# Who makes the low parts of the expert weights: GpSimd or VectorE

## The chip, the core and the metric

The kernel runs on one core of a Trainium2 chip. The core has TensorE (PE: matrix products, with PEld for loading the stationary operand), VectorE (DVE), ScalarE (ACT), GpSimd (POOL) and SyncE (SP), which work from queues of their own and wait for each other by semaphores. Each queue is taken strictly in order. The metric is the device time of one execution in microseconds; lower is better.

## The reference: what is computed

The program is a windowed attention over 8 batches (8 heads, 512 local and 32 global positions, head size 64), and behind it a layer of 8 experts. The attention's output is the matrix x of 4608 rows of 512. The routing is a capacity-limited one: all 4608 x 8 logits are taken from the largest down, and a token goes to the first expert that still has room (576 rows each).

```
logits = x @ w_gate
order = np.argsort(-logits.flatten())
for idx in order:
    tok, e = (int(idx) // E, int(idx) % E)
    if assigned[tok] >= 0 or counts[e] >= cap:
        continue
    assigned[tok] = e
    counts[e] += 1
...
for e in range(E):
    mask = assigned == e
    h = np.maximum(x[mask] @ w1[e], 0.0)
    out[mask] = h @ w2[e]
```

With w1[e] of 512 x 1024 and w2[e] of 1024 x 512, each expert costs two matrix products over 576 rows.

## The kernel before, in words

**Attention** comes first (about 235 us of the span), then the routing of the first expert alone, and then eight **phases**, one for each expert in the order in which experts fill up. `ffn(ph)` writes one phase. It has three stretches on TensorE:

- **H** (L851): 16 groups of 12 products, `hh = relu(w1 x)`, over 544 of the 576 rows and the rest in a small piece; 192 matmuls of 128x272. Each group is turned by ACT into `hh` (L853) and then by DVE into its low part `hl` (L405, out `hl`), and the PSUM buffer `H` (three of them) comes free when DVE is done.
- **P** (L869): 16 small matmuls for the last 32 rows.
- **Y** (L879): 4 tiles of 24 products against w2, 96 matmuls of 128x512, with two small ones (L885) behind the first tile. ACT takes each tile out (L824) and GpSimd scatters it to DRAM (L731).

**Split numbers.** To keep accuracy with the reduced-precision matmul type, each factor is used as a high and a low part, and a product is three matmuls (high x high, low x high, high x low). ACT makes the high part of a weight piece of 128x512 (`w1h`, `w2h`, L701, a copy to the reduced type), and another engine makes the low part `raw - high` (`w1l`, `w2l`, L702). Each expert has 8 pieces of w1 and 8 of w2. Before the change GpSimd makes the low parts, all but four pieces of the first expert, which DVE makes ahead of the phases.

**Weights and rows** arrive by indirect DMAs issued from GpSimd's queue: two of 1 MB for w1 (into `w1r`), two of 1 MB for w2 (into `w2r`), and five for the expert's rows of x (`xg`), which PE transposes (`trans_x`, L724), ACT copies (`xh`) and DVE splits (`xl`).

**Routing** of the next expert runs beside the phase. It is a chain that goes back and forth between PE and DVE. A search of 8 rounds finds the value at which an expert is full. A round is: 17 small matmuls and one more (`R`, L468) that count with the operand `r_G`; `r_ce` on DVE; two matmuls; the scan `r_pm` on DVE; and then the next `r_G`, a 128x544 operation on DVE. Behind the search come the expert's number (`widx`, which allows its weights to be fetched), the counts (`r_cs`, a matmul pair, `r_pos`), a compaction (`r_rhs`, `r_ohl`, 34 matmuls, `r_w`, one matmul) and the list of rows (`idx`, which allows `xg` to be fetched). The next search follows at once.

**What sets the order.** The program is written out ahead of time by a small planner in `experts`. `step(ns)` advances a clock `V.now` after every matmul; `Queue` (L383 to L406) adds an estimated cost for each DVE operation to `V.busy`; `routing` yields the value of `V.now` from which its next piece may be written; `todo` holds the other jobs with a time and a condition. In each `step` the first job that is due and whose condition holds is written, and then the routing goes on if its time has come. `calm` (L747) is the condition under which a low part may be written, and `pool_op` keeps the estimate for GpSimd's queue. So the places of matmuls, DVE operations and DMA issues in their queues come from these estimates, and the chip follows the queues.

Of the kernel before, what the change touches and what calls it, by code (L numbers as in the profile page):

```python
# [371 lines left out]
AHEAD = 200  # L372
# [10 lines left out]
class Queue:  # L383
# [12 lines left out]
    def __getattr__(s, name):  # L396
        op = getattr(s.eng, name)

        def issue(*args, **kw):
            aps = [x for x in list(args) + list(kw.values()) if hasattr(x, "dtype") and hasattr(x, "shape")]  # L400
            n = max(int(np.prod(x.shape[1:])) for x in aps)
            fast = name in ("tensor_scalar", "tensor_copy") or name == "tensor_tensor" and all(
                mybir.dt.size(x.dtype) == 2 for x in aps)
            s.busy = max(s.busy, s.now) + 130 + n * (0.55 if fast else 1.05)
            return op(*args, **kw)  # L405
        return issue  # L406

# [257 lines left out]
def experts(ctx, tc, A, xd, ident, rt, out):  # L665
    nc = tc.nc
# [33 lines left out]
    def split(hi, lo, raw, eng):  # L700
        nc.scalar.activation(hi, raw, AF.Copy)  # L701
        eng.tensor_tensor(lo, raw, hi, op=ALU.subtract)  # L702

    def split_w1(raws, j, eng):
        q = slice(512 * (j % 2), 512 * (j % 2) + 512)
        split(w1h[j // 2][:, q], w1l[j // 2][:, q], raws[j // 4][:, (j // 2) % 2, q], eng)

    def split_w2(j, eng):
        split(w2h[j], w2l[j], w2r[j // 4][:, j % 4], eng)
# [24 lines left out]
    V = rt.V  # L734
    V.now = V.busy = 0.0
    pool, dma, need = [0.0], [0.0], [0.0]
    fill, todo, raw1 = [], [], {}
    done, cur, mid, wrote = [False], [0], [-1], [0.0]

    def pool_op(ns, nbytes=0):  # L740
        pool[0] = max(pool[0], V.now) + ns
        if nbytes:
            dma[0] = max(dma[0], pool[0] + 1800) + nbytes / 360.0
            return dma[0] + 300
        return pool[0]

    def calm():  # L747
        return pool[0] < V.now + AHEAD

    def chain():  # L750
        for ph in range(1, E):
# [37 lines left out]
            bubble()  # L789

    def low1(p, j):
        split_w1(raw1[p], j, nc.gpsimd)
        pool_op(1225)

    def low2(j):
        split_w2(j, nc.gpsimd)
        pool_op(1225)

    def get_w1(p, half):
        raw1[p] = load_w1(p)  # L800
        r = [pool_op(1040, 1 << 20) for _ in range(2)]
        for i in range(4):
            at(f"a{p}", r[i // 2], lambda j=2 * i: low1(p, j), lambda: (half or mid[0] == p - 1) and calm())
        for i in range(4):
            at(f"b{p}", r[i // 2], lambda j=2 * i + 1: low1(p, j), lambda: mid[0] == p - 1 and calm())
# [7 lines left out]
    def get_w2(p):  # L813
        load_w2(p)
        r = [pool_op(1040, 1 << 20) for _ in range(2)]
        for j in range(8):
            at(f"w{p}", r[j // 4], lambda j=j: low2(j), lambda: cur[0] == p and calm())
# [93 lines left out]
    for j in range(4):  # L911
        at("b0", 0, lambda j=j: low1(0, 2 * j + 1), calm)
    for j in range(8):
        at("w0", 0, lambda j=j: low2(j), calm)
# [80 lines left out]
```

## Time and profile before

| | us |
|---|---|
| median of three timed runs | 792.48 (790.07 to 793.71) |
| the profiled execution, its own time | 788.45 |
| span of that execution | 786.7 |
| TensorE busy, by the page | 715.7 (91%) |
| VectorE busy | 487.2 (62%) |
| ScalarE busy | 312.9 (40%) |
| GpSimd busy | 319.6 (41%) |
| mean granted TensorE clock | 0.947 |

Times in the profile are counted from the start of the span. The first product of the first expert's H is at 276.7 us and the last product of the last expert's Y at 774.3. A "phase" below is the time from one expert's first H product to the next one's.

### The profile page before, as it was taken

Reading aid. Unit: us, or ns where it says so; the run is one execution under the profiler, and the core shown is the slowest. Engines: PE = TensorE matmul, PEld = TensorE weight load, DVE = VectorE, ACT = ScalarE, POOL = GpSimd, SP = SyncE. Lnnn points to the kernel's source line nnn. Section 1 sums busy time; section 2 is a strip of 40 time slices with the busy share of each in tenths; the row PEclk is TensorE's granted clock in tenths of the full one; section 3 lists DMA queues with packets and bytes.
Section 4 is the critical chain, followed back from the end, with each engine's and each line's share of the span. In section 5 each row is a group of like instructions: output and inputs, shape, how many; then the busy total and the mean of one; then the engine's idle time right before and its main releaser. Section 6 shows DMA issues by size and latency. Waiting matters only on the chain.

```text
span 786.7 us, 21184 instructions
## 1 busy us (share of the span) xinstructions
PE 715.7 (91%) x8636; PEld 579.5 (74%) x8636; DVE 487.2 (62%) x1705; ACT 312.9 (40%) x849; POOL 319.6 (41%) x314
## 2 busy tenths in 40 slices
PE   7999999999983499979997997999799999999993
PEld 6777777777751488769777876977777887988973
DVE  5887886778777887787758657666774731130210
ACT  4657675665640242342422423332331423443410
POOL 5221111111000471782746645553644655574510
PEclk9999999999995589998998999899999989999998
DMA  9999789878420520602332323132142313341000
GB/s 350 409 353 339 295 298 321 299 276 310 162 70 1 164 108 30 256 31 83 126 108 105 125 102 134 43 136 85 68 127 82 121 49 137 129 137 72 28 26 31
DMA packets 32417, 120.51 MB, mean 153 GB/s; under 512 B 6720, under 2 KB 6976, under 8 KB 24128
## 3 DMA queue, kind: packets, MB, share of 16 engines
q1 hardware_dynamic: 22080, 67.78, 23.2%
q0 software_dynamic: 10240, 51.39, 18.7%
q8 instruction: 68, 1.11, 0.6%
q14 instruction: 29, 0.24, 0.1%
HBM read 101.32 MB, written 17.83 MB: 151 GB/s over the span
## 4 chain that ended last, share of the span: by engine, by line
PE 79%; DVE 14%; issue 2%; DMA 2%; ACT 1%; POOL 0%; POOLq 0%; SPq 0%; ACTq 0%; DVEq 0%
PE Y L879 21%; PE H L851 21%; PE S L134 8%; PE R L468 6%; PE T L150 5%; PE O L162 4%; DVE r_G L405 3%; PE S L195 2%; PE T L259 2%; PE H L724 2%; PE Y L869 2%; PE O L234 2%; PE T L224 2%; DVE r_pos L405 1%; PE O L265 1%
## 5 line engine op out<-in xcount | busy, mean ns | idle before, releaser
L851 PE MATMUL H<-xh,w1h 128*128 128x272 f32 x512 | 156.3, 305 | 12.7 <-DVE hl L405 12.7
L851 PE MATMUL H<-xl,w1h 128*128 128x272 f32 x512 | 155.3, 303 | 0.0
L851 PE MATMUL H<-xh,w1l 128*128 128x272 f32 x512 | 154.5, 302 | 0.0
L405 DVE SCALAR_TENSOR_TENSOR hl<-H,hh 128x272 fp32r<-128x272 f32 x128 | 55.8, 437 | 119.4 <-ACT hh L853 80.0
L851 PEld LDWEIGHTS H<-xh,w1h 128*128 128x128 f32 x512 | 102.9, 201 | 14.3 <-DVE hl L405 13.8
L853 ACT ACTIVATE hh<-H 128x272 fp32r<-128x272 f32 x128 | 50.8, 397 | 155.3 <-PE H L851 154.0
L702 POOL TENSOR_TENSOR w2l<-w2r,w2h 128x512 fp32r<-128x512 f32 x64 | 82.8, 1315 | 63.1 <-ACT w2h L701 56.7
L145 ACT ACTIVATE p<-p,nm 128x128 f32<-128x128 f32 x256 | 81.7, 392 | 65.7 <-DVE ls L165 33.1
L879 PE MATMUL Y<-w2h,hh 128*128 128x512 f32 x256 | 103.6, 405 | 0.0
L879 PE MATMUL Y<-w2h,hl 128*128 128x512 f32 x256 | 103.4, 404 | 0.0
L879 PE MATMUL Y<-w2l,hh 128*128 128x512 f32 x256 | 103.2, 403 | 0.0
L851 PEld LDWEIGHTS H<-xl,w1h 128*128 128x128 f32 x512 | 102.6, 200 | 0.2
L851 PEld LDWEIGHTS H<-xh,w1l 128*128 128x128 f32 x512 | 102.7, 200 | 0.0
L86 POOL COPY qz<-q 64x544 f32<-64x544 f32 x60 | 38.2, 636 | 147.6 <-DMA q<-in_qk_dram 109.3
L702 POOL TENSOR_TENSOR w1l<-w1r,w1h 128x512 fp32r<-128x512 f32 x60 | 79.1, 1335 | 46.9 <-ACT w1h L701 46.5
L824 ACT ACTIVATE y<-Y 128x512 f32<-128x512 f32 (+1 forms) x40 | 23.4, 593 | 139.7 <-PE Y L879 90.2
L134 PE MATMUL S<-qk,qz 128*64 128x128 f32 x1024 | 71.2, 281 | 4.3 <-DVE qz L86 3.1
L731 POOL DMA_INDIRECT out_dram<-y,idx x40 | 40.9, 1022 | 71.8 <-ACT y L824 40.4
L134 PEld LDWEIGHTS S<-qk,qz 128*64 128x64 f32 x1024 | 55.5, 138 | 17.0 <-issue 13.4
L141 DVE CUSTOM_DVE_ANT_0 p<-S,mask 128x128 f32<-128x128 f32 x256 | 58.8, 285 | 7.7 <-PE S L134 3.5
L879 PEld LDWEIGHTS Y<-w2h,hh 128*128 128x128 f32 x256 | 48.3, 189 | 14.0 <-issue 5.0
L879 PEld LDWEIGHTS Y<-w2l,hh 128*128 128x128 f32 x256 | 48.4, 189 | 9.1
(164 smaller groups left out, 1236.2 us busy)
## 6 DMA issues: line engine op xcount, KB each, us to landing
vw<-in_vw_dram SPq DMA_DIRECT2D x32, 1040.0 KB, 7.8
qk<-in_qk_dram SPq DMA_DIRECT2D x32, 432.0 KB, 5.6
q<-in_qk_dram SPq DMA_DIRECT2D x32, 272.0 KB, 5.4
xd<-xs SPq DMA_DIRECT2D x8, 1024.0 KB, 6.6
xd<-xg SPq DMA_DIRECT2D x64, 8.0 KB, 5.7
xg<-xd,idx POOLq DMA_INDIRECT x40, 3.6
out_dram<-y,idx POOLq DMA_INDIRECT x40, 2.7
mask<-in_mask_dram SPq DMA_DIRECT2D x1, 512.0 KB, 5.7
```

The source lines that it names most:

```text
L86: eng.tensor_copy(z[r, :, h, :], q[r].rearrange("p (j i) -> p j i", i=32))
L134: nc.tensor.matmul(st[64 * r:64 * r + 64, c, :], z[:, j].rearrange("p h i -> p (h i)"), kw[:, k0:k0 + 128], start=True, stop=True)
L141: nc.vector.tensor_tensor_reduce(s.p[:, c, :], st[:, c, :], mask[:, 4 * s.u + c, :], 1.0, -BIG, ALU.add, ALU.max, nm[:, c:c + 1])
L145: nc.scalar.activation(s.p[:, c, :], s.p[:, c, :], AF.Exp, bias=nm[:, c:c + 1], scale=SCALE)
L150: nc.tensor.transpose(t[:, c, :], s.p[:, c, :], ident)
L405: return op(*args, **kw)
L468: s.nc.tensor.matmul(out, *args, **kw)
L702: eng.tensor_tensor(lo, raw, hi, op=ALU.subtract)
L731: nc.gpsimd.indirect_dma_start(out=out, out_offset=bass.IndirectOffsetOnAxis(ap=rt.idx[ph][:n, t:t + 1], axis=0), in_=y[:n], in_offset=None)
L851: nc.tensor.matmul(p, w[d][:, fs], x[:, d, q], start=(d + k == 0), stop=(d + k == 5))
L853: nc.scalar.activation(hh[:, f, q], p, AF.Relu)
L879: nc.tensor.matmul(p, h[:, f, q], w[f], start=(f + k == 0), stop=(f + k == 9))
```

## The change: what it does

Low parts are issued to the wrapped DVE queue `V` in place of GpSimd, so the planner counts their cost in `V.busy` and no longer in GpSimd's estimate. The condition `calm` asks about DVE's estimated queue instead of GpSimd's. The estimated cost of a scan on DVE is doubled (2.2 ns an element for 1.05).

```
-            s.busy = max(s.busy, s.now) + 130 + n * (0.55 if fast else 1.05)
+            s.busy = max(s.busy, s.now) + 130 + n * (2.2 if "scan" in name else 0.55 if fast else 1.05)
...
     def calm():
-        return pool[0] < V.now + AHEAD
+        return V.busy < V.now + AHEAD
...
     def low1(p, j):
-        split_w1(raw1[p], j, nc.gpsimd)
-        pool_op(1225)
+        split_w1(raw1[p], j, V)

     def low2(j):
-        split_w2(j, nc.gpsimd)
-        pool_op(1225)
+        split_w2(j, V)
```

124 low parts move from GpSimd's queue to DVE's, and because the planner works with the new estimates, the routing's pieces stand elsewhere too.

**GpSimd's queue, the issues for one expert (the fourth) before.** `w1l`, `w2l` are low parts, the DMA rows fetch weights (`w1r`, `w2r`) and rows of x (`xg`) and store results (`out_dram`):

```order
L685 DMA w1r<-in_w_dram,widx 128x2048 x2
L702 TENSOR_TENSOR w1l_4822<-w1r,w1h_4818 128x512
L702 TENSOR_TENSOR w1l_4823<-w1r,w1h_4819 128x512
L702 TENSOR_TENSOR w1l_4824<-w1r,w1h_4820 128x512
L702 TENSOR_TENSOR w1l_4825<-w1r,w1h_4821 128x512
L702 TENSOR_TENSOR w1l_4822<-w1r,w1h_4818 128x512
L685 DMA xg<-xd,idx 128x512 x4
L685 DMA xg<-xd,idx 32x512
L685 DMA w2r_4842<-in_w_dram,widx 128x2048
L685 DMA w2r_4843<-in_w_dram,widx 128x2048
```

Now, for the third expert, on the same queue:

```order
L685 DMA w1r<-in_w_dram,widx 128x2048 x2
L685 DMA w2r_4842<-in_w_dram,widx 128x2048
L685 DMA w2r_4843<-in_w_dram,widx 128x2048
L731 DMA out_dram<-y,idx 4352x512
L685 DMA xg<-xd,idx 128x512 x4
L685 DMA xg<-xd,idx 32x512
```

The low parts are gone from the queue, and the 2 MB of w2 now stand ahead of the rows `xg`; the second pair of fences below shows when these are wanted.

**DVE's queue in H of the second expert, a round of the search, before:**

```order
L405 SCALAR_TENSOR_TENSOR r_G<-r_x_6265,r_pm_6286,cf 128x544
L405 SCALAR_TENSOR_TENSOR hl<-H,hh 128x272
L405 TENSOR_SCALAR r_x_6331<-r_x_6265,r_pm_6286 128x34
L405 TENSOR_TENSOR r_ce<-R,dk 128x256
L405 SCALAR_TENSOR_TENSOR hl<-H,hh 128x272
L405 SCALAR_TENSOR_TENSOR r_pm_6353<-R_6329,fin 128x128
```

Now, at the same place:

```order
L405 SCALAR_TENSOR_TENSOR r_G<-r_x_6193,r_pm_6223,cf 128x544
L405 SCALAR_TENSOR_TENSOR hl<-H,hh 128x272
L405 TENSOR_TENSOR w2l_4836<-w2r_4842,w2h_4828 128x512
L405 TENSOR_SCALAR r_x_6273<-r_x_6193,r_pm_6223 128x34
L405 TENSOR_TENSOR r_ce<-R,dk 128x256
L405 SCALAR_TENSOR_TENSOR hl<-H,hh 128x272
L405 TENSOR_TENSOR w2l_4837<-w2r_4842,w2h_4829 128x512
L405 TENSOR_TENSOR w2l_4838<-w2r_4843,w2h_4830 128x512
L405 SCALAR_TENSOR_TENSOR r_pm_6301<-R_6271,fin 128x128
```

Between two steps of the chain stand one or two low parts more, and on TensorE the rounds stand 33 to 37 H products apart instead of 24; in Y they stay 14 products apart.

**TensorE's queue at the turn to the fourth expert, before:** the first of the five transposes of its rows stands behind the second product of Y.

```order
L869 MATMUL Y<-w2r_4842,h_4848 32x512 x2
L869 MATMUL Y<-w2r_4843,h_4848 32x512 x2
L879 MATMUL Y<-w2h_4826,hh 128x512
L879 MATMUL Y<-w2l_4834,hh 128x512
L724 MATMUL H<-ident,xg 128x128 x4
```

Now, at the turn to the third expert (the later turns up to the sixth are alike; lines behind L795 have shifted by two, so L877 is the Y product and L849 the H product):

```order
L724 MATMUL H<-ident,xg 128x128 x4
L877 MATMUL Y<-w2h_4832,hl 128x512
L877 MATMUL Y<-w2h_4833,hh 128x512
L877 MATMUL Y<-w2l_4841,hh 128x512
L724 MATMUL H<-ident,xg 128x128 x4
L877 MATMUL Y<-w2h_4833,hl 128x512
L724 MATMUL H<-ident,xg 128x128 x4
L724 MATMUL H<-ident,xg 128x32 x4
L849 MATMUL H<-xh,w1h_4818 128x272
```

The routing of the next expert now ends in Y: counted in Y products of the same phase, the matmul for `r_cs` stands behind product 35, the 34 matmuls behind product 58, the one for `idx` behind product 66, and the five transposes behind products 88, 92, 95, 96 and 96 of 96. Before, `idx` came behind product 31 of Y for the second expert, behind product 3 for the third, and in the H ahead of that Y for the fourth to the seventh. On DVE three low parts of w1, which need the weights just fetched, now stand ahead of `idx`.

## The prediction

> **What bounds the kernel now.** I read the page's slices first, then a table by stage, then the chain of waits, and last the timelines around its longest pieces. The table has a row for each of the eight phases and one for the tail; its columns are the stretch, its length, the busy time of each engine, the granted clock and DMA.
>
> ```profile
> core 0: us, PE busy (x) PEld busy (x) DVE busy (x) ACT busy (x) POOL busy (x), PEclk, DMA share, GB/s
> 276.70:341.90 65.20, 63.12 (x586) 52.21 (x586) 52.23 (x114) 23.34 (x56) 38.69 (x32) 0.97 0.31 117
> 341.90:408.90 67.00, 62.47 (x565) 51.45 (x564) 45.29 (x109) 21.37 (x51) 34.70 (x30) 0.95 0.29 101
> 408.90:476.00 67.10, 62.64 (x563) 52.15 (x562) 44.73 (x104) 21.49 (x51) 36.12 (x31) 0.95 0.29 101
> 476.00:543.00 67.00, 62.21 (x545) 51.77 (x544) 43.98 (x103) 21.50 (x51) 35.00 (x30) 0.95 0.29 97
> 543.00:612.00 69.00, 62.43 (x528) 52.21 (x527) 46.19 (x111) 21.48 (x51) 35.41 (x30) 0.95 0.28 94
> 612.00:674.70 62.70, 59.69 (x402) 52.09 (x401) 24.13 (x55) 21.48 (x51) 33.87 (x29) 0.95 0.29 99
> 674.70:725.70 51.00, 51.00 (x327) 44.73 (x326) 10.78 (x22) 21.26 (x51) 33.67 (x30) 1.00 0.37 127
> 725.70:774.80 49.10, 49.04 (x307) 42.67 (x305) 7.76 (x17) 14.56 (x38) 15.83 (x14) 1.00 0.08 29
> 774.80:786.70 11.90, 0.00 (x0) 0.00 (x0) 0.00 (x0) 0.60 (x1) 0.96 (x1) 0.68 0.06 22
> ```
>
> TensorE sets the pace in every phase, and the last two, which have no routing, are pure TensorE work. In the first six it idles (length minus PE busy) 2.1, 4.5, 4.5, 4.8, 6.6 and 3.0 us: 25.5 us. The clock is below 1 as well: the missing shares times the lengths (0.03 x 65.2, then 0.05 x 332.8) make 18.6 us, of which a part falls into the idle time. Where does one loss come from? Three engines' timelines, one event:
>
> ```profile
> 348.71 4.94 POOL L702 TENSOR_TENSOR w2l<-w2r,w2h 128x512 fp32r<-128x512 f32 x4
> 349.11 5.13 DVE L405 SCALAR_TENSOR_TENSOR r_G<-r_x,r_pm,cf 128x544 bf16<-128x544 f32 x1
> 349.60 0.29 PE L851 MATMUL H<-xh,w1l 128*128 128x272 f32 x1
> 354.30 0.30 PE L468 MATMUL R<-r_oh,r_G 128*32 128x16 bf16 x17 [4.15 <-DVE r_G L405]
> 355.17 0.43 PE L851 MATMUL H<-xl,w1h 128*128 128x272 f32 x1
> ...
> 242.07 0.78 DVE L405 SCALAR_TENSOR_TENSOR r_G<-r_x,r_pm,cf 128x544 bf16<-128x544 f32 x1
> ```
>
> The same `r_G` takes 0.78 us at 242 us, where GpSimd is idle, and 5.13 us here, ending when GpSimd's train of four low parts ends. TensorE, which needs it, idles 4.15 us, and its products then run with 0.43 us for 0.29: the clock has dropped. It happens again with `r_pos`, an operation on 34 elements a partition:
>
> ```profile
> 484.67 5.41 DVE L405 SCALAR_TENSOR_TENSOR r_pos<-r_a,r_a 128x34 int32<-128x34 f32 x1
> 485.08 4.94 POOL L702 TENSOR_TENSOR w2l<-w2r,w2h 128x512 fp32r<-128x512 f32 x4
> 490.49 0.59 PE L851 MATMUL H<-xh,w1h 128*128 128x272 f32 x1 [4.31 <-DVE hl L405]
> ```
>
> So the bound in the routed phases is a DVE operation with two operands in SBUF that waits for GpSimd's low parts. The Trainium skill (SBUF — State Buffer, "SBUF: two separate sides") says that the two engines share a port pair which one holds for a whole instruction while the other is fully blocked. By that, one instruction of 1.24 us (4.94/4) would be the most that `r_G` waits, and taking the low parts away would be worth a quarter of what I forecast, about 11 us; the rows show it waiting through four, so the measurement decides.
>
> **What the phases need without waits.** Unit prices from quiet stretches of the chain of waits (start, length, what):
>
> ```profile
> 674.83 24.05 PE H L851 x192
> 698.88 1.85 PE Y L869 x16
> 725.90 24.06 PE H L851 x192
> 757.58 0.47 PE Y L885 x2
> 709.20 16.70 PE Y L879 x72
> 528.61 1.90 PE Y L879 x8
> 530.50 0.38 PE R L468 x18
> 530.88 1.45 PE Y L879 x6
> 532.45 1.91 PE Y L879 x8
> 436.44 2.35 PE R L468 x35
> ```
>
> - A bare phase: 24.05 + 1.85 + 16.70 x 96/72 (22.27) + 0.47 = 48.64. Eight: 389.1.
> - The five transposes: the seventh phase lasts 725.90 - 674.83 = 51.07, so 2.43 more. Seven: 17.0.
> - A round of the search: 532.45 - 528.61 = 3.84 for 14 Y products of 0.232 (3.25), so 0.59. Six searches of eight: 28.3.
> - The end of a routing: 2.35 for the 34 matmuls, and about 0.45 (my estimate from a round's 0.38) for the small ones. Seven: 19.6.
>
> Sum 454.0, against 498.1 in the table (786.7 - 11.9 - 276.7): 44.1 us are lost: the 25.5 of idle time, and 18.6 in which the clock was low or waits were too short to show as idle. A microsecond of idle time goes with 1.7 lost (44.1/25.5).
>
> **The change, part by part.** *Removed:* 124 low parts on GpSimd (section 5 of the page has them as 64 and 60), and with them the waits above: -44.1. The chain of search rounds then has 0.78 for `r_G` everywhere. *Added:* the same 124 on DVE.
>
> ```profile
> 270.18 2.50 DVE L702 TENSOR_TENSOR w1l<-w1r,w1h 128x512 fp32r<-128x512 f32 x4
> 270.91 1.38 POOL L685 DMA_INDIRECT xg<-xd,idx  x1 [0.30 <-issue]
> 267.15 0.95 POOL L685 DMA_INDIRECT xg<-xd,idx  x1 [5.71 <-DVE idx L405]
> ```
>
> Each takes 2.50/4 = 0.625 us; 16 a phase are 10.0 us. DVE is busy 45.3 of 67.0 us in the second phase, and part of that is waiting for GpSimd; in a phase of about 60 us it will be at some 50, 83%. Is it hidden? Between a round's `r_ce` and its scan stand at most an `hl` and two low parts: 0.44 (the page's groups) + 1.25 = 1.7 us, then the scan with 0.42 and `r_G` with 0.78; with `r_ce` (0.42 in the groups) and 0.6 for the ways between the engines the round needs 3.9. The program gives 14 H products to the one step (1.75 us at 24.05/192) and 19 to 23 to the other (2.4 to 2.9), 4.1 or more. I take nothing for it, and with the cover gone 0.625 for each low part on the path. In Y no low parts stand among the rounds.
>
> *Moved:* the end of the routing. This is the tight place, since five row fetches must land before the next H. Durations of the first routing, which runs undisturbed:
>
> ```profile
> 256.93 0.42 DVE L405 TENSOR_TENSOR_SCAN r_pm<-R,fin 128x128 f32<-128x128 f32 x1 [0.46 <-PE R L468]
> 259.06 1.13 POOL L685 DMA_INDIRECT w1r<-in_w_dram,widx  x1 [64.21 <-DVE r_S L405]
> 264.96 1.15 ACT L701 ACTIVATE w1h<-w1r 128x512 fp32r<-128x512 f32 x2 [29.70 <-DMA w1r<-in_w_dram,widx]
> 268.24 1.15 ACT L701 ACTIVATE w1h<-w1r 128x512 fp32r<-128x512 f32 x2 [2.13 <-DMA w1r<-in_w_dram,widx]
> 270.55 0.66 PE L724 MATMUL H<-ident,xg 128*128 128x128 f32 x4 [0.15 <-DMA xg<-xd,idx]
> DMA to landing us min/median/max: 3.2/3.9/4.9
> ```
>
> Count from the start of Y. The last search step stands behind product 24, with two rounds before it: 5.6 + 1.2 = 6.8 us. In the rows the first issue for w1 comes 259.06 - 256.93 = 2.1 after the scan's start, so here at 9.2 with 0.3 for the two matmuls ahead of the scan. The first `w1r` lands 5.9 after its issue, at 15.1; the second 3.3 later (a MB takes that long here), at 18.4; the 2 MB of w2 at 25.0, if the queue is served in order. Low parts wait for `w1r` on DVE ahead of `idx`: the third needs the second landing, ACT's copy (1.15/2) and its own 0.625, so it ends at 19.6. `idx` can come behind product 66: 15.3, three rounds' inserts, the two small products and the 34 matmuls (about 5 together), 20.3; so the low parts are in time by 0.7, and what queues behind them (`r_w`, `idx`) would delay the fetches one for one if they weren't. The fetches start at 20.7 and, by 0.95 + 0.30, are 1.25 apart. The first lands at 20.7 + 3.9 = 24.6 by the last row (that of the first turn, with w2 ahead in the queue too), or at 25.8 if it stands behind w2; its transposes come at 20.3 + 22 x 0.232 = 25.4. The fifth is issued at 25.7 and lands near 29.4; its transposes come at 20.3 + 30 x 0.232 + 2.0 = 29.3. It just fits. I take 1 us of idle for each of six turns, 6; bounds 0 (all fits) and 3 (landing at 4.9, one low part and its copy late). For small waits that the unit prices don't hold I take 5, bounds 0 and 12 (the 18.6 less what the clock takes of it). The doubled scan estimate only spaces rounds.
>
> [...]
>
> **Sum.** 276.7 + 454.0 + 11.9 + 6 + 5 = 753.6 of span. The profiled execution's own time is 1.75 above its span, and the median of the timed runs 4.0 above that: 753.6 + 5.8 = **759.4**; I say 760.
>
> **Rivals.**
>
> 1. *Starved descriptors.* Each of the five fetches of a turn loses 0.43: 6 x 2.15 = 12.9, so 772. For it: the 1.38, and three low parts stand behind `idx` while the fetches are issued. Against it: it took a train of four to do that here, and there they stand singly between other work.
> 2. *Late data at the turn, slower than before.* If fetches land d later than the slack, TensorE idles d at each of six turns, and the clock drops behind a long idle time, as it did behind 349 us. Place: the transposes behind product 88. Price 6 x 1.7 x d: with d = 5 it is 51, in place of the 6, and the time 804. It decides from d near 3.8, where the 33 us of gain are eaten up. For it: 4 MB in one queue ahead of the rows, and no slack left in my sum. Against it: the sum, and landings of at most 4.9 with 2 MB ahead at the first turn.
> 3. *DVE becomes the bound.* If half of the 96 low parts of the first six phases fall on the path, 48 x 0.625 = 30: 789, no change. For it: 83% load. Against it: the spacing above.
> 4. *It doesn't do what it says:* the long DVE operations are not GpSimd's doing and remain, 790. Against it: 0.78 at 242 us, and in both events shown the stalled operation ends with the train.
>
> **How the numbers follow.** Forecast 70%, rival 1 14%, rival 2 8%, rival 3 5%, rival 4 3%. About half a per cent, 4 us, is what a measurement of this kernel can tell from no change. Faster is the forecast with rival 1, 0.84; within it rivals 3 and 4, 0.08; slower rival 2, 0.08. The range 751 to 782 holds both bounds of the turns and the small waits (the low one 742.6 + 5.8, and 2.6 for what never is zero) and rival 1 with a turn's 3 us; it leaves out rivals 2 to 4.
>
> **What would show it.** Right: no DVE operation near 5 us; `r_G` near 0.78 and `r_pos` below 1 everywhere; low parts 0.62 to 0.69 on DVE; granted clock 1.0 in the phases; the first six phases 60 to 62 us, the last two as before. Wrong: waits of 3 us or more at the transposes for `xg` (rival 2), GpSimd issues at 1.4 (rival 1), `R` matmuls waiting for `r_G` or `r_ce` behind low parts (rival 3). The forecast falls if the phases' idle time stays above 20 us.

## The result: 771.36 us, and the profile after

The change takes 771.36 us (769.70 to 772.52), the kernel before beside it 791.28 (788.69 to 793.71): a ratio of 0.9754, with a 95% interval of 0.9718 to 0.9791. It is faster, by 20 us where 32 were forecast. The profiled execution takes 769.70, its span is 767.9.

The table by stage for the kernel after, its eight phases (stretch, length, busy time of each engine, granted clock, DMA share, GB/s):

```profile
core 0: us, PE busy (x) PEld busy (x) DVE busy (x) ACT busy (x) POOL busy (x), PEclk, DMA share, GB/s
275.40:336.50 61.10, 60.89 (x527) 51.51 (x525) 44.37 (x117) 21.90 (x53) 10.79 (x12) 0.96 0.34 124
336.50:397.50 61.00, 59.89 (x526) 49.37 (x525) 42.93 (x115) 22.15 (x53) 15.03 (x14) 1.00 0.30 107
397.50:460.50 63.00, 60.40 (x525) 49.49 (x525) 43.29 (x116) 21.53 (x52) 14.68 (x14) 1.00 0.30 103
460.50:523.40 62.90, 60.37 (x524) 49.43 (x524) 43.20 (x116) 21.48 (x52) 14.63 (x14) 1.00 0.29 103
523.40:587.80 64.40, 60.55 (x525) 49.44 (x525) 43.29 (x116) 21.58 (x52) 14.97 (x15) 1.00 0.29 101
587.80:651.50 63.70, 60.60 (x526) 49.37 (x526) 43.20 (x115) 22.55 (x54) 16.47 (x16) 1.00 0.30 104
651.50:706.40 54.90, 54.32 (x361) 47.29 (x362) 21.96 (x43) 21.15 (x52) 14.02 (x14) 1.00 0.35 125
706.40:755.90 49.50, 49.23 (x307) 42.73 (x305) 12.33 (x25) 14.46 (x38) 4.77 (x5) 1.00 0.06 23
```

The phases take 480.5 us where they took 498.1. In the first six TensorE idles 13.4 us (25.5 before), and the granted clock is 1.00 in all but the first. The groups of the low parts and of the operation that used to stall:

```profile
L405 DVE TENSOR_TENSOR w2l<-w2r,w2h 128x512 fp32r<-128x512 f32 x64 | 42.7, 689 | 37.2 <-ACT w2h L701 36.7
L405 DVE TENSOR_TENSOR w1l<-w1r,w1h 128x512 fp32r<-128x512 f32 x60 | 40.0, 687 | 22.7 <-ACT w1h L701 22.5
L405 DVE SCALAR_TENSOR_TENSOR r_G<-r_x,r_pm,cf 128x544 bf16<-128x544 f32 x42 | 33.0, 786 | 1.5
L405 DVE SCALAR_TENSOR_TENSOR r_pos<-r_a,r_a 128x34 int32<-128x34 f32 x7 | 1.4, 195 | 0.2
```

`r_G` has a mean of 0.786 us and `r_pos` of 0.195; nothing near 5 us is left. The stalls behind GpSimd are gone. What holds TensorE now is in the table of its waits (engine, line, waited for: us in total, times, longest), first of its products and then of its weight loads:

```profile
PE H L849 <- DVE hl L405: 10.7, 20, 0.8
PE H L724 <- DMA xg<-xd,idx: 4.0, 5, 1.2
PE H L849 <- DVE xl L405: 1.4, 5, 0.4
...
PEld H L849 <- DVE hl L405: 8.7, 11, 0.9
```

10.7 us on products and 8.7 on loads, none longer than 0.9. The two overlap for 6.3 us, so TensorE waits 13.1 us for `hl`. Of the 4.0 us for `xg`, 2.5 lie ahead of 275.4, before the first phase. One wait for `hl`, at the start of the fourth H, in the timeline of the kernel after (start, us, engine, operation, and in brackets the idle time before it and what ended it):

```profile
462.73 0.40 ACT L851 ACTIVATE hh<-H 128x272 fp32r<-128x272 f32 x1 [1.87 <-PE H L849]
463.02 1.14 ACT L701 ACTIVATE w1h<-w1r 128x512 fp32r<-128x512 f32 x2
463.68 1.29 DVE L405 TENSOR_TENSOR w1l<-w1r,w1h 128x512 fp32r<-128x512 f32 x2 [0.83 <-ACT w1h L701]
...
464.89 0.42 DVE L405 TENSOR_TENSOR_SCAN r_pm<-R,fin 128x128 f32<-128x128 f32 x1
465.34 0.79 DVE L405 SCALAR_TENSOR_TENSOR r_G<-r_hi,r_pm,cf 128x544 bf16<-128x544 int32 x1
...
466.05 0.78 DVE L405 SCALAR_TENSOR_TENSOR hl<-H,hh 128x272 fp32r<-128x272 f32 x2
466.53 0.39 PE L849 MATMUL H<-xh,w1h 128*128 128x272 f32 x1 [0.64 <-DVE hl L405]
```

ACT has turned the first group into `hh` by 463.13. Its `hl` could run then, but in DVE's queue stand, ahead of it, a low part whose high part ACT is still making (until 463.65), a second low part, the scan and `r_G`. The first of the two `hl` ends at 466.48, 3.35 us after `hh`; only then is that PSUM buffer free, and TensorE, which has filled the other two in the meantime, has stood still for 0.64 us.

The other remainder is the turn. The same view, between the third and the fourth expert:

```profile
395.83 0.47 PE L877 MATMUL Y<-w2h,hl 128*128 128x512 f32 x1
396.25 0.99 PE L724 MATMUL H<-ident,xg 128*128 128x128 f32 x8
396.75 0.69 DVE L405 TENSOR_TENSOR xl<-H,xh 128x512 fp32r<-128x512 f32 x1 [0.44 <-ACT xh L726]
397.09 0.77 ACT L726 ACTIVATE xh<-H 128x512 fp32r<-128x512 f32 x2
397.49 0.39 PE L849 MATMUL H<-xh,w1h 128*128 128x272 f32 x1 [0.25 <-DVE xl L405]
```

Y's last product starts at 395.83; transposes still follow it, and behind them copies and splits, so H starts at 397.49, 1.66 later, where a product's distance in Y is 0.232. Five of the first six turns are like this one; at the first it is 1.12.

Measured against the prediction's own unit prices, the 26.5 us that the phases lie above the 454.0 split like this. *H stretches* of the first six: 184.1 for 6 x (24.05 + 6 rounds x 0.59) = 165.5, so 18.6. *Y and turns* of the first six: 376.1 - 184.1 = 192.0 for 6 x (1.85 + 22.27 + 0.47 + 2.43 + 2 x 0.59 + 2.8) = 186.0, so 6.0. *The last two phases*: 1.9.

### The profile page after: what moved, and what is told of

It is laid out like the page before. It is cut to its first block, busy times and chain, and to the rows that moved or that the text cites. A ratio compares the mean times of both kernels' runs of the same rounds, so it can differ in the third digit from the quotient of the medians.

```text
span 767.9 us, 21120 instructions
## 1 busy us (share of the span) xinstructions
PE 708.8 (92%) x8636; PEld 568.8 (74%) x8636; DVE 506.8 (66%) x1829; ACT 313.1 (41%) x849; POOL 162.2 (21%) x190
## 4 chain that ended last, share of the span: by engine, by line
PE 47%; DVE 7%; DMA 3%; issue 3%; ACT 3%; POOL 0%; POOLq 0%; ACTq 0%; DVEq 0%
PE Y L877 20%; PE H L849 18%; PE R L468 5%; DMA xg<-xd,idx 2%; PE Y L867 2%; DVE w2l L405 2%; PE H L724 2%; DVE r_G L405 1%; ACT w2h L701 1%; DMA w1r<-in_w_dram,widx 1%; DVE hl L405 1%; DVE w1l L405 1%; DVE r_pm L405 1%; ACT w1h L701 0%; DVE xl L405 0%
## 5 line engine op out<-in xcount | busy, mean ns | idle before, releaser
L849 PE MATMUL H<-xh,w1h 128*128 128x272 f32 x512 | 152.8, 298 | 12.7 <-DVE hl L405 10.7
L849 PE MATMUL H<-xh,w1l 128*128 128x272 f32 x512 | 150.6, 294 | 0.0
L849 PE MATMUL H<-xl,w1h 128*128 128x272 f32 x512 | 149.9, 293 | 0.0
L849 PEld LDWEIGHTS H<-xh,w1h 128*128 128x128 f32 x512 | 97.3, 190 | 17.8 <-DVE hl L405 8.7
L877 PE MATMUL Y<-w2h,hh 128*128 128x512 f32 x256 | 103.3, 403 | 0.0
L877 PE MATMUL Y<-w2h,hl 128*128 128x512 f32 x256 | 102.8, 401 | 0.0
L877 PE MATMUL Y<-w2l,hh 128*128 128x512 f32 x256 | 102.6, 401 | 0.0
L849 PEld LDWEIGHTS H<-xl,w1h 128*128 128x128 f32 x512 | 97.6, 191 | 0.0
L849 PEld LDWEIGHTS H<-xh,w1l 128*128 128x128 f32 x512 | 97.4, 190 | 0.0
L685 POOL DMA_INDIRECT w1r<-in_w_dram,widx x16 | 16.2, 1013 | 268.0 <-DVE r_a L405 160.9
L405 DVE SCALAR_TENSOR_TENSOR hl<-H,hh 128x272 fp32r<-128x272 f32 x128 | 53.6, 434 | 25.9 <-ACT h L853 15.3
L405 DVE TENSOR_TENSOR w2l<-w2r,w2h 128x512 fp32r<-128x512 f32 x64 | 42.7, 689 | 37.2 <-ACT w2h L701 36.7
L877 PEld LDWEIGHTS Y<-w2h,hh 128*128 128x128 f32 x256 | 48.2, 188 | 16.0 <-issue 5.9
L701 ACT ACTIVATE w1h<-w1r 128x512 fp32r<-128x512 f32 x64 | 36.7, 623 | 46.4 <-DMA w1r<-in_w_dram,widx 46.2
```

What stands on the lines that cost most here:

```text
L849: nc.tensor.matmul(p, w[d][:, fs], x[:, d, q], start=(d + k == 0), stop=(d + k == 5))
L877: nc.tensor.matmul(p, h[:, f, q], w[f], start=(f + k == 0), stop=(f + k == 9))
```

## The experiments

All were timed beside the kernel before. It took 791.17 us on the chip of the first four, 803.47 on that of the next four, 802.90 on that of the last four.

| kernel | us, median (lowest to highest) | ratio to before, 95% interval |
|---|---|---|
| e1: memsets in place of GpSimd's low parts | 754.53 (753.56 to 755.74) | 0.9528 (0.9495 to 0.9560) |
| e2: change, scan estimate as before | 757.70 (757.41 to 762.50) | 0.9588 (0.9544 to 0.9632) |
| e3: change, `hl` first | 753.92 (752.48 to 757.61) | 0.9528 (0.9485 to 0.9571) |
| e4: change, low parts 1 us late | 760.58 (759.69 to 763.61) | 0.9618 (0.9582 to 0.9654) |
| e5: change, 4 H and 2 Y buffers | 757.99 (756.27 to 759.75) | 0.9421 (0.9366 to 0.9475) |
| e6: e2 and e3 together | 758.13 (757.21 to 760.13) | 0.9436 (0.9382 to 0.9491) |
| e7: e6 with 4 H and 2 Y buffers | 762.28 (759.99 to 763.50) | 0.9472 (0.9417 to 0.9526) |
| e8: before, scan edit alone | 801.53 (796.88 to 804.64) | 0.9980 (0.9948 to 1.0011) |
| e9: the change again | 773.46 (772.49 to 773.53) | 0.9635 (0.9589 to 0.9681) |
| e10: e5 again | 755.96 (754.42 to 760.58) | 0.9410 (0.9362 to 0.9459) |
| e11: e2 with 4 H and 2 Y buffers | 756.65 (754.34 to 757.37) | 0.9417 (0.9369 to 0.9466) |
| e12: e3 again | 758.06 (755.79 to 759.62) | 0.9436 (0.9386 to 0.9486) |

### Is the cause of the old stall what both engines read? (e1)

```
-        eng.tensor_tensor(lo, raw, hi, op=ALU.subtract)
+        if eng is nc.gpsimd:
+            eng.memset(lo.bitcast(F32), 0.0)
+        else:
+            eng.tensor_tensor(lo, raw, hi, op=ALU.subtract)
```

> The kernel before, in its own order; each of the 124 low parts on GpSimd is replaced by a memset of the same tile in the same place of the same queue. It leaves out the subtraction (the low parts of the weights are zero on GpSimd's pieces). Theory (GpSimd's low parts block DVE because both engines read two operands from SBUF): a memset reads nothing, so r_G is at 0.78 us and r_pos below 1 everywhere, the idle time of 25 us in the first six phases falls to below 8, and the time comes to 748 to 756, since before's order has fewer low parts beside the rounds than the change has. Rival (any GpSimd work of 128x512 on SBUF blocks DVE, whatever it reads): r_G still waits through the trains, up to about four times one memset, and the time stays above 770.

Measured: 754.53, and TensorE idles 2.5 us in the first six phases; both as the theory expected. `r_G` in this kernel (durations min/median/max, then the first and last start), and one that runs beside memsets, in its timeline:

```profile
L405 DVE SCALAR_TENSOR_TENSOR r_G<-r_x,r_pm,cf x42: 783/785/789, 244.4 to 578.5; 128x544 bf16<-128x544 f32 x42
```

```profile
402.22 1.93 POOL L703 MEMSET w2l<- 128x512 f32 x4
402.26 0.42 DVE L405 TENSOR_TENSOR_SCAN r_pm<-R,fin 128x128 f32<-128x128 f32 x1 [1.26 <-PE R L468]
402.72 0.78 DVE L405 SCALAR_TENSOR_TENSOR r_G<-r_x,r_pm,cf 128x544 bf16<-128x544 f32 x1
403.42 0.78 DVE L405 TENSOR_SCALAR r_x<-r_x,r_pm 128x34 f32<-128x34 f32 x1
```

The theory holds: with GpSimd writing the same tiles at the same place of its queue, but reading nothing, `r_G` is never above 0.789; the one shown lies within a train of four memsets from its start to its end. The run also tests the 454.0 of the unit prices without any work added to DVE: its phases come to 462.2. But the third row shows something that neither theory had: `r_x`, an operation with a single tile as source that takes 0.235 elsewhere, takes 0.78 here and ends when the memsets do. The last section comes back to it.

### What does the scan's estimate do? (e2, e8)

```
-            s.busy = max(s.busy, s.now) + 130 + n * (2.2 if "scan" in name else 0.55 if fast else 1.05)
+            s.busy = max(s.busy, s.now) + 130 + n * (0.55 if fast else 1.05)
```

> The change without its edit of the scan's estimate (1.05 ns an element as before): low parts on DVE, rounds of the search written as far apart as before's planner would. Theory (the missing 12 us are DVE's queue: hl stands behind the scan, r_G and low parts and frees the H buffers late): rounds closer together put more of the chain's steps on the path, and the time is 772 to 785. Rival (the spacing of the rounds is too wide or does not matter, the 26 us of loss have another place): 765 to 772. If the wide spacing is itself what costs, because the end of the routing then comes too late, 760 to 765.

> The kernel before with only the edit of the scan's estimate (2.2 ns an element for 1.05); low parts stay on GpSimd. Theory (the stalls of r_G and r_pos behind GpSimd's trains rule here, and rounds written somewhat farther apart hide a part of them): 780 to 792. Rival (the edit costs by itself wherever it stands, as the 13.7 us between the change and the change without it): 798 or more.

Without the edit the change takes 757.70, 13.7 less than with it (771.36, beside a kernel before of the same speed). The rows of sums over the six H stretches, for the kernel after and for e2:

```profile
sum 184.10, PE 173.65 PEld 160.53 DVE 135.10 ACT 74.57 POOL 15.11; mean PE 28.94 PEld 26.75 DVE 22.52 ACT 12.43 POOL 2.52
```

```profile
sum 176.00, PE 171.48 PEld 159.64 DVE 132.65 ACT 75.02 POOL 12.90; mean PE 28.58 PEld 26.61 DVE 22.11 ACT 12.50 POOL 2.15
```

8.1 us less in H; and by the same stretches 186.8 in Y and the turns, 5.2 less. The code and the order of the queues give a reason for both, which was not tested by itself. A scan counts 147 ns longer (128 x 1.15) in `V.busy`, so `step` finds `V.busy < V.now` more rarely and `hl` is written later: from the end of `hh` to the end of its `hl`, taken from the two rows of each of the first 96 groups, the median is 2.06 us after the change and 1.64 in e2. And the rounds stand farther apart (in Y 14 products for 10), so that the list of rows stands behind product 66 of Y instead of 57, and the last two of a turn's five transposes, which in e2 all stand within Y, fall behind its end: from Y's last product to the first of H it is 0.23 us at every turn of e2.

In e2, theory 1 had expected the opposite sign: rounds closer together were to cost. The third case, wide spacing being the cost, has the right sign, but 757.70 lies below its 760 to 765, and its reason, the late end of the routing, covers only the 5.2 us at the turns and not the 8.1 in H. Alone on the kernel before (e8) the edit changes nothing that can be measured, 801.53 to 803.47. Both cases of e8 were reckoned for a kernel before of 791 us, so their ranges decide nothing here; a cost of 13.7 us wherever the edit stands is ruled out by the interval of the ratio. GpSimd's stalls are there as before: `r_G` takes up to 3.5 us, and `r_pos` up to 4.4.

```profile
L405 DVE SCALAR_TENSOR_TENSOR r_G<-r_x,r_pm,cf x42: 783/786/3523, 240.9 to 608.7; 128x544 bf16<-128x544 f32 x42
```

### hl earlier in DVE's queue (e3, e12), and low parts later (e4)

In e3, `step` writes the waiting `hl` once 700 ns have passed since its group, ahead of jobs from `todo`:

```
+    due = [0.0]
...
         V.now += ns
+        if fill and V.now >= due[0]:
+            bubble()
...
+                due[0] = V.now + 700
```

> The change, with hl written on DVE from 700 ns after its group's last product, ahead of waiting low parts. Theory 1 (of the 26 us of loss in the phases about 20 are TensorE waiting for an H buffer that hl frees too late, because hl is written last): TensorE's waits for hl, 10.7 us on products and 8.7 on loads, fall below 5, the H stretches shorten by 1 to 2 us each in the first six phases, time 755 to 764. Theory 2 (hl is late because the head of DVE's queue waits for ScalarE's casts, 59 us in all in this trace): hl still stands behind low parts that wait, and the time stays within 767 to 772. Rival (DVE's load itself is the bound): 769 to 776.

In e4, ACT's cast is written where it was, but the low part 1 us later, as a job of its own:

```
-        eng.tensor_tensor(lo, raw, hi, op=ALU.subtract)
+        if tag:
+            at(tag, V.now + LATE, lambda: eng.tensor_tensor(lo, raw, hi, op=ALU.subtract), calm)
+        else:
+            eng.tensor_tensor(lo, raw, hi, op=ALU.subtract)
```

> The change, with each low part written on DVE 1 us after its high part was written on ScalarE, so that DVE's head of queue finds the cast done. Theory 2 (hl is late because the head of DVE's queue waits for ScalarE's casts): DVE's waits for w1h and w2h, 59 us, fall below 20, TensorE's waits for hl fall below 8, and the time is 757 to 765. Theory 1 (hl's own place in the order is the cause): the waits for the casts fall, but the time stays at 767 to 772. Rival (low parts that come later are needed by TensorE before they are done): PE waits for w1l or w2l appear and the time is above 774.

e3 takes 753.92 and e4 760.58. In e3 products wait 0.7 us for `hl` in all, and loads 1.4:

```profile
PE H L852 <- DVE hl L405: 0.7, 3, 0.2
```

The H stretches come to 174.9 and Y with the turns to 188.7. In e4 DVE's waits for casts fall from 59.2 us to 16.7, and what is left is a single wait of 16.6, which the change has too (16.5); TensorE's waits for `hl` fall to 4.1 (1.1 and 3.0), the H stretches to 175.3.

```profile
PE H L853 <- DVE hl L406: 1.1, 1, 1.1
...
PEld H L853 <- DVE hl L406: 3.0, 8, 1.4
...
DVE w2l L406 <- ACT w2h L702: 16.6, 1, 16.6
```

So theory 1 and theory 2 each find what they expect of their own remedy (e3 lies 1 us below its range), and each is wrong about the other's, which was to stay at 767 to 772: `hl` is late for its place in the order and because DVE's queue waits for ACT, and taking away either is enough for most of it. Neither comes near the times of the two rivals. Neither run settles that it is the PSUM buffer through which a late `hl` costs, since both also move the rounds and with them the list of rows (behind products 41 to 62 of Y, for 59 to 66). e12 takes 758.06 where e9, the change, takes 773.46:

> The kernel with hl written first, beside the change on one chip: 14 to 18 us below the change, 753 to 757 where the change takes 771. If the single look of the first call was the chip's, less than 10 below.

15.4 below, as expected. In the profiled executions 3.9 of the 4.3 us between e12 and e3 lie in the seventh phase, 55.4 us for 51.5: a load there waits 2.4 us for a high part of w1, and a product beside it 2.2 for `hl`, which e3 does not show. Why that high part is late stays open.

### The buffer by itself (e5, e9, e10)

```
-                p = ps.tile([128, HF], F32, name="H", bufs=3)
+                p = ps.tile([128, HF], F32, name="H", bufs=4)
...
-            p = ps.tile([128, DM], F32, name="Y", bufs=3)
+            p = ps.tile([128, DM], F32, name="Y", bufs=2)
```

> The change with four PSUM buffers for H and two for Y in place of three and three; the order of the instructions on every engine stays that of the change, only what the products wait for differs. Theory (in the H stretches the loss is H buffers that hl frees too late): TensorE's waits for hl, 10.7 us on products and 8.7 on loads in the run of the change, fall below 6, the first six H stretches shorten by 1 to 2 us each, the Y stretches and turns stay, and the time is 760 to 765. Rival (hl only ends a wait whose cause is the routing chain, so that TensorE would wait for the next thing in its queue just as long): waits move from hl to r_G, r_ce or r_pm, and the time stays at 768 to 773. If two Y buffers are too few, the Y stretches grow by more than 1 us each.

> The change itself, so that the next three are compared with it on one chip. The kernel before took 791 us on the chip of the first four experiments and 803 on that of the second four, and the change was only timed beside the 791. Theory (the difference of 12 us belongs to the stalls of the kernel before, which depend on when GpSimd's trains meet DVE's operations): 769 to 774 on any chip. Rival (such a chip runs everything slower): 771 times the ratio of the kernel before here to 791.

> The kernel with four H and two Y buffers, beside the change on one chip. Theory (H buffers freed late): 12 to 15 us below the change measured beside it, all of it in the H stretches. Rival (the 13 us between two chips were the chip): less than 5 us below.

e5 takes 757.99, 2 us below its range, on a chip on which the change was not timed; e9 and e10 are the pair to read. e9 lies within the 769 to 774 of its theory. e10 takes 755.96 where e9 takes 773.46, 17.5 us less, with every instruction in the same place of its queue. The sums over the six H stretches, of e9 and then of e10:

```profile
sum 185.70, PE 174.28 PEld 160.94 DVE 135.36 ACT 74.38 POOL 14.72; mean PE 29.05 PEld 26.82 DVE 22.56 ACT 12.40 POOL 2.45
```

```profile
sum 169.30, PE 169.08 PEld 159.08 DVE 136.17 ACT 76.40 POOL 15.12; mean PE 28.18 PEld 26.51 DVE 22.69 ACT 12.73 POOL 2.52
```

16.4 us less in H, 3.8 above the 165.5 of the unit prices; TensorE's waits for `hl` go from 14.6 us (11.7 on products and 9.6 on loads, 6.7 of them at the same time) to a single one of 1.3, which stands in the seventh phase. Y with the turns comes to 192.4 for 191.2: loads now wait 5.5 us for one of the two Y buffers. The profiled executions differ by less than the medians, 11.9 us: that of e10 is the slowest of its four (760.58), its phases begin 2 us later, and its last two take 1.2 more. And the event of the result section in e10, at the same place of the same H:

```profile
460.89 0.40 ACT L851 ACTIVATE hh<-H 128x272 fp32r<-128x272 f32 x1 [2.04 <-PE H L849]
461.84 1.29 DVE L405 TENSOR_TENSOR w1l<-w1r,w1h 128x512 fp32r<-128x512 f32 x2 [0.56 <-ACT w1h L701]
463.05 0.42 DVE L405 TENSOR_TENSOR_SCAN r_pm<-R,fin 128x128 f32<-128x128 f32 x1
463.50 0.79 DVE L405 SCALAR_TENSOR_TENSOR r_G<-r_hi,r_pm,cf 128x544 bf16<-128x544 int32 x1
464.21 0.78 DVE L405 SCALAR_TENSOR_TENSOR hl<-H,hh 128x272 fp32r<-128x272 f32 x2
464.23 0.29 PE L849 MATMUL H<-xh,w1l 128*128 128x272 f32 x1
```

The first `hl` ends 3.35 us behind `hh` (461.29 to 464.64), as late as before, and TensorE's products go on at their usual distance beside it. DVE is busy as long as before in these stretches (136.2 for 135.4). So neither DVE's load nor the lateness costs time by itself. A group takes 24.05/16 = 1.5 us; by that, as an estimate, three buffers bear a lateness of two groups less ACT's part, 3.0 - 0.4 = 2.6 us, and a fourth bears 1.5 more. The rivals of e5 and e10 (the wait moves to another place; the chip made the difference) fall.

e9 also shows where the chips differ: the change takes 773.46 where the kernel before takes 802.90, and 771.36 where it takes 791.28. The kernel before is 11.6 slower there, the change 2.1. That fits stalls which depend on when trains and operations meet, but no trace of the kernel before was taken on that chip, so it isn't shown.

### Do the remedies add up? (e6, e7, e11)

> The change without its edit of the scan's estimate and with hl written from 700 ns after its group: both of the single edits, which gave 757.7 and 753.9. Theory (both take the same lateness away, hl behind the rounds and the end of the routing behind Y's second half): little is left to gain, 749 to 754, over a floor of 748.4 that the unit prices give (742.6 of span and 5.8). Rival (two separate causes, 13.7 and 17.4 us, that add up): 740 to 746. Rival (rounds closer together collide with low parts on DVE): 757 or more.

> The kernel of scan estimate as before and hl first, with four H buffers and two Y buffers. Theory (hl late only matters through the H buffers): with hl already early the fourth buffer is worth less than 2 us, 748 to 753. Rival (buffers are short even with hl early): 3 us or more below the same kernel with three.

> The change without the scan's estimate and with four H and two Y buffers. Theory: the first six H stretches come from 29.3 to about 28.0, the Y stretches grow by 0.5 to 1 for the two buffers, so 3 to 6 us below the 757.7 of the same kernel with three, 752 to 755 on a chip where the change takes 771. Rival (two Y buffers cost as much as the fourth H buffer gives): 757 or more.

They don't. e6 takes 758.13, 4 us above the 749 to 754 of its theory and no less than e12 with one of its two edits, on a chip where the kernel before takes as long. Its H stretches are shorter (172.7), but Y and the turns come to 192.7. The searches now end within H from the fourth phase on, and rounds of the next one fall into Y; TensorE waits once 2.2 us for `r_ce`. Its second rival (rounds that collide with low parts) gives 757 or more, which fits, but which waits make up the 192.7 was not followed further, so its mechanism isn't shown. In e7 the H stretches stay at 172.6: with `hl` early the fourth buffer gives nothing, as theory said. But the time is 762.28 and not 748 to 753, 4 us above e6 on the same chip, from which only the buffers differ: Y and the turns take 197.8 for 192.7, and loads in Y wait 4.9 us for ACT to take out one of the two Y buffers. They cost in e11 too (its waits, of products and of loads):

```profile
PE Y L877 <- ACT y L822: 2.1, 8, 0.3
...
PEld Y L877 <- ACT y L822: 6.2, 8, 0.8
```

There the H stretches fall to 169.5, 28.2 each, and Y with the turns grows from 186.8 to 191.0, 0.7 each: both as expected, but together they leave little, and 756.65 lies between the two cases. On the last chip e10, e11 and e12 lie at 755.96 to 758.06 with ranges that overlap: any of the three remedies makes a kernel that is 15 to 17.5 us below the change, and these runs don't separate them.

## Why the prediction was right, and where it was not

**The bound and what is removed: right.** Stalls of `r_G` and `r_pos` were the cause, they are gone, and e1 shows that it takes operands that GpSimd reads. That DVE waits through whole trains holds for the longest stalls alone (see the last section).

**The need of 454.0: borne out as a floor.** No kernel came below it; e1 (462.2) and e3 (464.0) came within 10 us.

**The turns: the size right by luck.** 6 were forecast and 6.0 measured. The forecast was for waiting for `xg`. In TensorE's timeline of the kernel after, that comes to 1.5 us in two waits, the only ones within the phases:

```profile
585.71 0.66 PE L724 MATMUL H<-ident,xg 128*128 128x128 f32 x4 [1.16 <-DMA xg<-xd,idx]
646.91 0.66 PE L724 MATMUL H<-ident,xg 128*128 128x128 f32 x4 [0.38 <-DMA xg<-xd,idx]
```

The rest goes with the transposes, copies and splits that stand behind Y's last product and that nothing covers (0.23 us from Y to H in e2, 1.66 here). The forecast had no term for them.

**"I take nothing for it", of the low parts on DVE, and the 5 for small waits: wrong, and here lies the miss.** What the forecast called small waits measures 18.6 in H and 1.9 in the last phases, 20.5 for 5 and far above the upper bound of 12. A fourth buffer for H takes 16.4 us out of H (e9 and e10). The cover was reckoned for the chain of the search alone: what stands between `r_ce` and the scan. `hl` figured in it only as one more operation that delays the chain. That something waits for `hl` itself, namely the next group but two, which needs its PSUM buffer, stood in the description of the kernel and in no sum. The event shown delays `hl` by 3.35 us behind `hh`, and three buffers bear about 2.7 (3.35 less the 0.64 that TensorE waited). Two of the forecast's signs failed: the third to the sixth phase take 62.9 to 64.4 us and not 60 to 62, and the seventh, into which the end of the last routing has moved, 54.9 and not 51.0 as before.

**"The doubled scan estimate only spaces rounds": wrong.** It was priced at nothing and costs 13.7 us. 8.1 of them lie in H, where the waits for `hl` fall from 13.1 us to 6.6 without it; this isn't a second loss beside the one above, it is a large part of it. The 5.2 at the turns lie in the place for which the forecast took its 6, since it counted from product 66, where this estimate puts the list of rows. The change without it comes out at 757.70, near the forecast of 759.4, but by another sum: 10.5 us above the need in H and 0.8 at the turns, where the forecast had 5 and 6.

**The sum.** 759.4, 15.5 more of losses (26.5 for 11), 1.3 less because the phases started at 275.4, 0.1 for the tail, and 2.3 less because the median lies 1.7 above the profiled execution and not 4.0: 771.4.

**The rivals.** Starved descriptors (rival 1) give nearly the measured time, 772, for a reason that isn't there: the 40 issues for `xg` have a median of 0.949 us, where this rival needs 1.38.

```profile
L685 POOL DMA_INDIRECT xg<-xd,idx x40: 877/949/1370, 266.0 to 670.3; - x40
```

Late data (rival 2) did not come: the longest wait of a product for `xg` is 1.2. *DVE becomes the bound* (rival 3) is nearest in mechanism, but not by load: DVE is busy 43.2 of 62.9 us in the fourth phase, 69% and not the 83% forecast, since the busy time before contained the stalls. It is the order in DVE's queue against the number of buffers.

## What to carry to other kernels

When work is added to an engine's queue, list everything on that engine for which another engine waits, not only the chain you are watching: each such operation has its own slack, and a PSUM buffer's slack is the number of buffers less one, times the time of a group, less what the engines ahead of the operation take (here some 2.7 us with three buffers and groups of 1.5). An estimate in a planner is an edit like any other; here one constant cost 13.7 us of the 33.5 that its neighbour gave, and one run without it tells. And the same loss can be cut in several places (order, waits at a queue's head, one buffer), but only once.

## What the runs showed of the hardware that was not expected

In e1 GpSimd's memsets read nothing, and yet they hold up operations of DVE that have a single tile as source. The low parts did this too (`r_x` took up to 1.27 us beside them, and `r_hl` 1.21); new is that it happens without any read. From the timeline of e1:

```profile
528.44 0.20 DVE L405 SCALAR_TENSOR_TENSOR r_pos<-r_a,r_a 128x34 int32<-128x34 f32 x1
...
528.90 3.62 DVE L405 TENSOR_SCALAR r_hl<-r_pos 128x34 int32<-128x34 int32 x2
529.07 3.45 DVE L405 SCALAR_TENSOR_TENSOR r_asgv<-r_a,vs,r_asgv 128x34 f32<-128x34 f32 x1
529.12 3.34 POOL L703 MEMSET w2l<- 128x512 f32 x7
532.56 0.20 DVE L405 CAST r_hb<-r_hl 128x68 bf16<-128x68 int32 x1
```

`r_hl`, one tile of 34 elements in and one out, takes 0.18 us where GpSimd is idle and 3.60 here, through a train of seven memsets, to its end. `r_asgv`, right behind it in the queue, ends with it; whether it waits by itself no trace shows. `r_G` and `r_pos`, with two tiles of SBUF as source, are not held up by memsets (`r_pos` keeps its 0.195 us) and are held up by low parts; `hl`, `r_ce` and the scan, which read PSUM, are held up by neither (`hl` has 0.42 to 0.44 us beside the low parts in the kernel before). The Trainium skill (SBUF — State Buffer, "SBUF: two separate sides") makes just this distinction: an operation with two SBUF inputs conflicts only with a GpSimd operation that reads SBUF, one in a two-port mode with any. The runs agree, with 0.784 to 0.787 for `r_G` beside memsets and up to 3.60 for `r_hl`; which of DVE's operations ran in such a mode no trace shows. They differ in one point: by the page the pair is held for one instruction, and here DVE waited for whole trains, four low parts (4.94 us) and seven memsets (3.34).

In the kernel before this was the exception, and it is where the time went. From the first phase on 44 of DVE's operations take over 0.25 us longer than others of their kind. 39 of them lose at most 1.1 us, less than one low part takes (1.24), one loses 1.6, and four, two `r_G` and two `r_pos`, lose 4.2 to 5.2 through trains of three or four low parts. But behind these four TensorE idles 16.7 of its 25.5 us in the first six phases. Why DVE gets its turn after one instruction at most times and not at these four, no run shows. The prediction's estimate for waits of one instruction was some 11 us; without the edit of the scan the change is worth 33.5.
